# Four shared PSUM banks and other places for attention steps and decoding in a fused attention and Mish-MLP kernel

## The chip, the cores and the metric

The kernel runs on one core of a Trainium2 chip. The metric is the device time of one execution in microseconds (us); each figure for a kernel is the median of several runs. The engines are TensorE (PE, with its weight loads PEld), VectorE (DVE), ScalarE (ACT), GpSimd (POOL) and SyncE (SP), which here only issues DMAs.

## The reference

Four batches of eight heads go through attention with rotary embedding (576 positions, 64 wide). The result, 2304 tokens by 512, goes through two matrix products with h * tanh(softplus(h)), Mish, between them.

```python
q_rot, k_rot = (rotate(q), rotate(k))
scores = scale * np.matmul(q_rot, k_rot.transpose(0, 1, 3, 2))
scores = scores - np.max(scores, axis=-1, keepdims=True)
attn = np.exp(scores)
attn = attn / (np.sum(attn, axis=-1, keepdims=True) + 1e-09)
x = np.matmul(attn, v)            # then (batch, position) x (head, width): 2304 x 512
h = x @ w_in                      # 512 x 2048
sp = np.where(h > 20.0, h, np.log1p(np.exp(np.minimum(h, 20.0))))
return ((h * np.tanh(sp)) @ w_out).astype(np.float32)   # 2048 x 512
```

## The kernel before, in words

Two heads make a pair; there are 16 pairs, four for each batch (pairs 0 to 3 are batch 0). A pair is worked on in five **steps** of 128 queries (the last one has 64 of either head). A step computes scores on PE into tag psc (L494, L488), their maxima on DVE (L502), exp on ACT (L504), and the inverse sums on DVE (L513, L515). For pairs 4 to 15 the weights are split into a high and a low fp16 part (L519 on POOL or L521 on ACT, then L525 on DVE) and transposed by a DMA from SP's queue (L603, L615, L618). For pairs 0 to 3 they stay fp32 and PE transposes them (L537, L550, L554; copies at L544, L545, L558 to L562). The product with V comes for each half of a pair (`av`, L632 to L645; L666, L668 write the fp16 parts of x).

The MLP takes each batch as two **chunks** of 256 and 320 tokens (chunks 0 to 7). A chunk has 16 **units** of 12 matmuls with W_in (`h_unit`, L866) with Mish on ACT (L871), eight splits of the result into fp16 parts (`h_split`, L881 on ACT or L882 on DVE, then L885 on DVE), and 16 **quarter sums** of 12 matmuls with W_out (`p_sub`, L900); four of them fill one output tile (L908).

The weights arrive as 64-bit words and are **decoded** in 32 blocks of 512 columns (`decode`: L762 and L765 or L764, then L768, L771 on DVE, L774, L778), after a scale from the largest exponent has been passed across the partitions by two small matmuls (`max_exponent`, L368, L374). ACT holds either its exp table or its Mish table; each change is an ACT_TABLE_LOAD.

All instructions are recorded first and then put in order by `Plan.order`: a list scheduler that gives each engine its ready instruction of the least priority. The priority is the place in the recorded program, plus shifts (`WSH`, `PSH`), less `ALPHA` times the length of the chain behind it; `DWELL` and `PEN` say how long ACT keeps its table. The recorded program is laid out by tables: `FRONT` attention steps come first, then `SLOTS[c]` names the places in chunk c at which one more step is recorded; `W1L`, `W1S`, `W1D` and `W2L`, `W2D` say at which step the loads, scales and decoding of the quarters of W_in and W_out are recorded, and `PREP`, `PRE0` how long ahead of its first step a pair is loaded.

PSUM has eight banks. Tag psc has two tiles of two banks each. Before, tag ph has two banks (transposes, weight blocks, units of W_in), pp one (sums of W_out, the fifth transposed block, scale exchanges), and po one (products with V). In the last two chunks every second unit and output tile also uses psc and po.

## Time and profile before

| | |
|---|---|
| median of 3 runs | 687.98 us (687.70 to 688.62) |
| the profiled execution's own time | 690.88 us |
| its span, first to last instruction | 688.7 us |
| PE busy | 605.8 us |
| ACT busy | 482.1 us |
| DVE busy | 445.5 us |
| POOL busy | 264.3 us |
| mean granted TensorE clock | 0.958 |

A share of busy time is a mean over stages with different limits, so a table of windows says more than the page's first lines. In it PEclk is the granted TensorE clock as a share of full speed. A wait names the instruction that sat idle and the one that released it. Lines such as L504 are lines of the kernel before.

### The profile page before, as it was taken

The page shows a single profiled execution, that of the slowest core. Times are in us where ns is not written, and L with a number is a line of the kernel's source. Part 1 is how long each engine was busy: PE and PEld are TensorE (multiplying, and loading weights), DVE is VectorE, ACT ScalarE, POOL GpSimd, SP SyncE. Part 2 cuts the span into 40 slices and gives each one's busy share as a digit, 9 for nine tenths or more (in the row PEclk, how much of TensorE's full clock was granted, in tenths as well). Part 3 has the DMA queues.
Part 4 walks back from the last instruction along what each step waited for, and adds up shares of the span by engine and source line. Part 5 has one row for each costly group of instructions (what it writes and reads, how often), then busy time and mean ns, then how long its engine had stood idle before and what let it go on. Part 6 is the DMA issues. An engine that isn't in the chain of part 4 may idle for free.

```text
span 688.7 us, 13057 instructions
## 1 busy us (share of the span) xinstructions
PE 605.8 (88%) x5028; PEld 448.4 (65%) x5028; DVE 445.5 (65%) x984; ACT 482.1 (70%) x864; POOL 264.3 (38%) x247
## 2 busy tenths in 40 slices
PE   1587688768998998968889999998999999999997
PEld 1354355545676676647778777677787767888775
DVE  4899897794887787676757767776767467211110
ACT  3587788764789897647999987779967756442420
POOL 5588734246354537566234546541212001000000
PEclk9868898899999999989999999999999999999999
DMA  9954423242269456896548465755365337100000
GB/s 364 421 188 129 152 68 97 86 147 70 81 142 213 82 119 148 180 202 156 89 88 180 111 121 134 165 88 106 61 122 82 80 62 153 32 2 16 16 11 29
DMA packets 143533, 82.50 MB, mean 120 GB/s; under 512 B 129264, under 2 KB 133488, under 8 KB 141936
## 3 DMA queue, kind: packets, MB, share of 16 engines
q1 hardware_dynamic: 138864, 76.96, 45.5%
q10 hardware_dynamic: 4608, 4.72, 2.0%
q8 instruction: 39, 0.64, 0.4%
q14 instruction: 22, 0.18, 0.1%
HBM read 45.09 MB, written 4.72 MB: 72 GB/s over the span
## 4 chain that ended last, share of the span: by engine, by line
PE 41%; ACT 8%; DMA 7%; DVE 3%; issue 1%; SPq 1%; POOL 1%; ACTq 0%; DVEq 0%; POOLq 0%
PE pp L900 15%; PE ph L866 12%; DMA et<-ew 5%; PE psc L494 4%; PE po L900 3%; PE psc L866 3%; PE po L644 2%; ACT e L504 2%; DMA stg<-in_vflat 1%; ACT L504 1%; ACT L871 1%; DVE ew L525 1%; DVE mx L502 1%; ACT mh L871 1%; PE po L640 1%
## 5 line engine op out<-in xcount | busy, mean ns | idle before, releaser
L866 PE MATMUL ph<-xt,w 128*128 128x256 f16 (+1 forms) x1344 | 180.8, 291 | 13.5 <-ACT mh L871 10.8
L866 PEld LDWEIGHTS <-w 128*128 128x128 f16 x1536 | 149.9, 99 | 59.5 <-issue 18.5
L900 PE MATMUL pp<-g,w 128*128 128x256 f16 (+1 forms) x1344 | 178.0, 287 | 1.9 <-ACT ot L908 1.8
L900 PEld LDWEIGHTS <-w 128*128 128x128 f16 x1536 | 148.0, 98 | 44.9 <-issue 7.9
L504 ACT ACTIVATE e<-psc,mx 128x576 f32<-128x576 f32 x144 | 105.5, 736 | 26.9 <-DVE mx L502 23.6
L502 DVE TENSOR_REDUCE mx<-psc 128x1 f32<-128x576 f32 x144 | 103.7, 750 | 31.3 <-PE psc L494 28.1
L525 DVE SCALAR_TENSOR_TENSOR ew<-e,rs,ew 128x576 f16<-128x576 f32 x108 | 100.3, 945 | 29.2 <-POOL ew L519 20.0
L519 POOL TENSOR_SCALAR ew<-e,rs 128x576 f16<-128x576 f32 x62 | 50.0, 811 | 178.7 <-DVE rs L515 108.4
L494 PE MATMUL psc<-qk 64*128 64x288 f32 (+1 forms) x736 | 90.6, 368 | 27.8 <-ACT qk L420 16.3
L398 POOL TENSOR_TENSOR raw<-raw,cs 128x576 f32<-128x576 f32 x60 | 91.2, 1535 | 58.3 <-DMA raw<-in_qk 55.6
L885 DVE SCALAR_TENSOR_TENSOR g<-mh,cells,g 128x512 f16<-128x512 f32 (+1 forms) x64 | 57.2, 894 | 75.0 <-ACT g L881 74.6
L494 PEld LDWEIGHTS psc<-qk 64*128 64x128 f32 (+1 forms) x736 | 60.2, 199 | 50.7 <-ACT e L504 17.2
L871 ACT ACTIVATE mh<-ph,cells 128x256 f32<-128x256 f32 (+1 forms) x112 | 53.2, 497 | 32.6 <-PE ph L866 31.9
L504 ACT ACT_TABLE_LOAD x43 | 55.2, 1283 | 7.2 <-DVE mx L502 6.5
L871 ACT ACT_TABLE_LOAD x44 | 56.5, 1283 | 1.2 <-ACT ot L908 0.4
L521 ACT ACTIVATE ew<-e,rs 128x576 f16<-128x576 f32 x46 | 35.1, 773 | 31.2 <-DMA et<-ew 22.8
L513 DVE TENSOR_SCALAR sm<-sm 128x1 f32<-128x1 f32 x144 | 21.2, 149 | 42.4 <-ACT e L504 42.0
L778 POOL TENSOR_TENSOR w<-mr,w 128x512 f16<-128x512 f32 x24 | 28.1, 1175 | 48.1 <-ACT w L774 48.0
L402 POOL TENSOR_TENSOR raw<-raw 128x288 f32<-128x288 f32 x48 | 45.2, 958 | 0.1
L645 PE MATMUL po<-et,v 128*64 128x256 f16 (+1 forms) x288 | 42.1, 299 | 0.0
L644 PE MATMUL po<-et,v 128*64 128x256 f16 (+1 forms) x288 | 42.1, 299 | 0.0
L537 PE MATMUL ph<-ident,e 128*128 128x128 f32 (+1 forms) x160 | 25.9, 299 | 15.1 <-ACT e L504 9.0
(113 smaller groups left out, 750.9 us busy)
## 6 DMA issues: line engine op xcount, KB each, us to landing
raw<-in_qk SPq DMA_DIRECT2D x32, 576.0 KB, 4.4
w<-in_w_in SPq DMA_DIRECT2D x4, 1024.0 KB, 12.6
stg<-in_v SPq DMA_DIRECT2D x12, 320.0 KB, 3.4
stg<-in_vflat SPq DMA_DIRECT2D x9, 384.0 KB, 3.4
w<-in_w_out SPq DMA_DIRECT2D x3, 1024.0 KB, 6.3
out_dram<-ot ACTq DMA_DIRECT2D x16, 160.0 KB, 2.1
g<-in_w_in SPq DMA_DIRECT2D x2, 1024.0 KB, 9.3
xt<-in_w_out SPq DMA_DIRECT2D x2, 1024.0 KB, 4.9
```

Of the source, the lines that this page charges most:

```text
L398: e.tensor_tensor(out=t()[:, :, s], in0=t()[:, :, s], in1=cs()[:, :, s], op=ALU.mult)
L402: e.tensor_tensor(out=to, in0=t()[:, 0, s], in1=t()[:, 1, s], op=ALU.add)
L494: nc.tensor.matmul(out, x[own, q], y[own, s], **kw)
L502: op((DVE, dve_ns(S), lambda: nc.vector.tensor_reduce(m(), pt()[:, :, :HS], axis=AX.XY, op=ALU.max, negate=True)), w=[m], r=[pt])
L504: op((ACT, act_ns(S, psum=True, ptr=2), lambda: nc.scalar.activation(e().rearrange("p (c s) -> p c s", c=2), pt()[:, :, :HS], AF.Exp, bias ...
L519: op([(POOL, 1.27 * S, lambda: nc.gpsimd.tensor_scalar(w()[:, c], e(), r()[:, h:h + 1], 1.0, op0=ALU.mult, op1=ALU.mult), 1), (ACT, act_ns ...
L525: op((DVE, dve_ns(S) + 61, lambda: nc.vector.scalar_tensor_tensor(out=w()[:, c], in0=e(), scalar=r()[:, h:h + 1], in1=w()[:, hc], op0=ALU. ...
L644: nc.tensor.matmul(po()[0:64, :n], V()[:, vi, c, 0:64], et[:, c, :], start=False, stop=last)
L866: nc.tensor.matmul(hp(), w1()[:, wi, cc, f:f + 128], x()[:, xi, cc, q0:q0 + n], start=cc == 0 and a == 0, stop=cc == NCC - 1 and a == 2)
L871: op((ACT, act_ns(n, psum=True, ptr=1), lambda j=j, hp=hp: nc.scalar.activation(hn()[:, j, :n], hp(), AF.Mish, scale=uh())), w=[(hn, j)], ...
L885: op((DVE, dve_ns(2 * n) + 61, lambda: nc.vector.scalar_tensor_tensor(out=g()[:, 1, f, :n], in0=hn()[:, :, :n], scalar=f32(gs), in1=g()[:, ...
L900: nc.tensor.matmul(pp()[:, :n], w2e[e]()[:, wi, f], g()[:, gi, f % 8, :n], start=f == 0 and a == 0, stop=f == NF - 1 and a == 2)
```

## The change

The tags ph, pp and po go. Four tiles of one bank each are made once (`bank0` to `bank3`), and `bank()` hands out one of them when the plan issues the first instruction that uses it: the one whose last user ends first by the plan. Units of W_in and weight blocks ask for `bank(1)`: they are issued only while one more bank than they take is free. A new output tile of W_out waits for the one before it (in chunks 6 and 7 for the one before that), as the single bank of pp made it wait. A decoding step is also held until the buffer that it decodes into is free. The tables have new numbers; where the decoding and the steps come to stand follows from them and from the plan.

```diff
-W1L = [1, 2, 3, 4]
-W1S = [2, 3, 4, 5]
-W1D = [3, 4, 6, 7]
+W1L = [2, 0, 1, 4]
+W1S = [2, 3, 6, 7]
+W1D = [5, 3, 7, 7]
-PRE0 = 2
-WSH = 17
-FRONT = 10
+PRE0 = 0
+WSH = 10
+FRONT = 11
-ALPHA = 26
-SLOTS = [[3, 7, 7, 11, 11, 15, 17, 19, 21, 23, 25, 27, 29, 30],
+ALPHA = 36
+SLOTS = [
+    [1, 8, 9, 12, 13, 17, 20, 21, 23, 27, 28, 31],
...
-DWELL = 2000
-PEN = 20
+DWELL = 2251
+PEN = 8
...
+    def pick(self, tag, keep=0):
+        b = Buf(lambda: self.free[tag][b.slot]())
+        b.ring = tag, keep
+        return b
...
         def room(bufs):
+            at = 0.0
+            for tag in {b.ring[0] for b in bufs}:
+                n = sum(b.ring[0] == tag for b in bufs) + max(b.ring[1] for b in bufs)
+                ends = sorted(until(x) for x in held[tag])
+                at = max(at, ends[n - 1])
             return at
...
                     for b in ops[n]["takes"]:
-                        taken[b.ring[0]].append(b)
+                        x = held[b.ring[0]]
+                        b.slot = min(range(len(x)), key=lambda i: until(x[i]))
+                        x[b.slot] = b
...
+    def bank(keep=0):
+        return plan.pick("bank", keep)
...
+    plan.free["bank"] = [Buf(lambda i=i: ps.tile([128, 512], F32, name=f"bank{i}")) for i in range(4)]
...
-            pt = psum((128, 512), "ph", 2)
+            pt = bank()
...
-        po = psum((128, 320), "po")
+        po = bank()
...
-        f, o = psum((128, 512), "ph", 2), row512()
+        f, o = bank(1), row512()
...
-            ph = psum((128, 2, 512), "psc", 2) if wide else psum((128, 512), "ph", 2)
+            ph = psum((128, 2, 512), "psc", 2) if wide else bank(1)
...
         if s == 0:
-            ml["pp"] = psum((128, 320), "po") if c >= 6 and e % 2 else psum((128, 320), "pp")
+            ml["pp"] = bank()
+            sums.append(ml["pp"])
+            ml["pp"].before = sums[-3:-2] if c >= 6 else sums[-2:-1]
```

Three places show how instructions move. The lines of the changed kernel stand 13 lower than those of before from `max_exponent` on (L502 of before is its L515, L768 its L781, L871 its L884), and 15 lower from the sums of `p_sub` on.

**First place: ACT at the start of the program.** The names are qk for the rotated query and key, g and w for the homes of raw weights, ph or bank for PSUM, cells for scales, e for exponentials. Before, and then after:

```order
L994 ACT_TABLE_LOAD
L765 ACTIVATE g_85<-g_85 128x512 x2
L420 ACTIVATE qk<-qk 128x576
L765 ACTIVATE g_87<-g_87 128x512
L504 ACTIVATE e_132,sm<-psc,mx 128x576
L504 ACTIVATE e_136,sm<-psc,mx 128x576
```

```order
L1009 ACT_TABLE_LOAD
L778 ACTIVATE w_69<-w_69 128x512 x2
L775 ACTIVATE bank_76<-w_69,cells 128x512
L775 ACTIVATE bank_77<-w_69,cells 128x512
L433 ACTIVATE qk<-qk 128x576
L787 ACTIVATE w_68<-mr 128x512
L778 ACTIVATE g_94<-g_94 128x512
```

The query's scaling (L420, now L433), which the first scores need, stands behind two weight blocks that are already being decoded with a scale.

**Second place: DVE from the maximum of pair 2's last step on.** The first row is that maximum. The rows go on to the next step's maximum (pair 3, step 2), which comes after 42 rows before and after 16 now. The first twelve of before, and the first twelve after:

```order
L502 TENSOR_REDUCE mx<-psc 128x1
L778 TENSOR_TENSOR w_69<-mr,w_69 128x512
L768 SCALAR_TENSOR_TENSOR ph<-ph,w_69 128x512
L427 SCALAR_TENSOR_TENSOR qk<-raw,qk 128x576
L689 TENSOR_REDUCE cells<-stg 128x1
L885 SCALAR_TENSOR_TENSOR g_1362<-mh,cells,g_1362 128x2x256
L689 TENSOR_REDUCE cells<-stg 128x1
L771 SCALAR_TENSOR_TENSOR mr<-w_69,ph 128x512
L365 TENSOR_REDUCE cells<-cells 128x1
L768 SCALAR_TENSOR_TENSOR ph<-ph,w_69 128x512
L771 SCALAR_TENSOR_TENSOR mr<-w_69,ph 128x512
L721 TENSOR_REDUCE cells<-stg 128x1
```

```order
L515 TENSOR_REDUCE mx<-psc 128x1
L526 TENSOR_SCALAR sm<-sm 128x1
L734 TENSOR_REDUCE cells<-w_69 128x1
L528 RECIPROCAL rs<-sm 128x1
L558 COPY et<-bank_76 128x4x128
L378 TENSOR_REDUCE cells<-cells 128x1
L558 COPY et<-bank_75 128x4x128
L383 TENSOR_REDUCE cells<-bank_76 1x1
L572 COPY et<-bank_77 128x128
L371 TENSOR_SCALAR cells<-cells 1x1
L575 COPY ew<-bank_77 128x128
L371 TENSOR_SCALAR cells<-cells 1x1
```

Decoding (L768, L771, L778) and the MLP's splits (L885) of before stand there no longer; the step's own sums and copies follow at once.

**Third place: ACT in chunk 4.** mh is a unit's Mish, g its split, e an exponential. Before, and then after:

```order
L871 ACTIVATE mh<-ph,cells 128x256 x2
L908 ACTIVATE ot<-pp,cells 128x320
L881 ACTIVATE g_5484<-mh,cells 128x2x256
L504 ACT_TABLE_LOAD
L504 ACTIVATE e_5588,sm<-psc,mx 128x576
L871 ACT_TABLE_LOAD
L871 ACTIVATE mh<-ph,cells 128x256 x2
L504 ACT_TABLE_LOAD
L504 ACTIVATE e_5643,sm<-psc,mx 128x576
L871 ACT_TABLE_LOAD
L871 ACTIVATE mh<-ph,cells 128x256 x2
```

```order
L517 ACT_TABLE_LOAD
L517 ACTIVATE e_5302,sm<-psc,mx 128x576
L517 ACTIVATE e_5331,sm<-psc,mx 128x576
L884 ACT_TABLE_LOAD
L884 ACTIVATE mh<-bank_77,cells 128x256
L884 ACTIVATE mh<-bank_75,cells 128x256
L894 ACTIVATE g_5298<-mh,cells 128x2x256
L884 ACTIVATE mh<-bank_76,cells 128x256
L679 ACTIVATE xt_70<-bank_74 128x320
L894 ACTIVATE g_5298<-mh,cells 128x2x256
L884 ACTIVATE mh<-bank_77,cells 128x256
```

One step's exponentials stand between every two Mish before; now several units follow each other under one table. Over the program ACT has 88 table loads before and 66 now.

## Rows read from the trace of the kernel before

**Rows 1.** The page, part 1: engine, busy us (share of the span), instructions.

```profile
PE 605.8 (88%) x5028; PEld 448.4 (65%) x5028; DVE 445.5 (65%) x984; ACT 482.1 (70%) x864; POOL 264.3 (38%) x247
```

**Rows 2.** Windows: from:to, us, busy of five engines, PEclk, DMA share, GB/s.

```profile
12.50:96.00 83.50, 60.12 (x362) 36.94 (x363) 76.14 (x195) 59.40 (x128) 57.23 (x54) 0.82 0.58 216
96.00:188.00 92.00, 72.70 (x549) 50.39 (x548) 69.51 (x174) 67.23 (x126) 40.39 (x36) 0.93 0.28 92
188.00:303.00 115.00, 105.37 (x896) 75.83 (x895) 86.93 (x191) 92.60 (x168) 63.78 (x55) 0.97 0.69 151
303.00:350.00 47.00, 39.54 (x363) 32.25 (x364) 34.01 (x68) 38.52 (x68) 18.36 (x17) 0.93 0.69 140
350.00:595.00 245.00, 238.01 (x2129) 182.44 (x2129) 162.01 (x337) 191.81 (x326) 78.12 (x76) 1.00 0.53 108
595.00:688.70 93.70, 90.09 (x735) 70.50 (x733) 12.07 (x15) 29.49 (x51) 0.00 (x0) 1.00 0.04 15
```

**Rows 3.** PE's waits, first from 303 to 350, then from 350 to 595 us.

```profile
PE psc L494 <- ACT e L504: 4.4, 3, 2.2
PE ph L866 <- ACT mh L871: 3.4, 4, 1.6
...
PE ph L866 <- ACT mh L871: 4.4, 5, 1.5
```

**Rows 4.** PE's timeline: start, us, engine, line, operation, count [idle before].

```profile
12.52 2.29 PE L494 MATMUL psc<-qk 64*128 64x288 f32 x8 [12.52 <-ACT qk L420]
...
187.94 1.06 PE L494 MATMUL psc<-qk 64*128 64x288 f32 x12
...
303.15 0.40 PE L494 MATMUL psc<-qk 64*128 64x288 f32 x1 [2.25 <-ACT e L504]
...
602.63 2.78 PE L866 MATMUL psc<-xt,w 128*128 128x256 f16 x24
605.26 1.47 PE L866 MATMUL ph<-xt,w 128*128 128x256 f16 x12
```

**Rows 5.** Groups by line: line, engine, operation, shapes, count, busy us, mean ns.

```profile
L768 DVE SCALAR_TENSOR_TENSOR ph<-ph,w 128x512 uint32<-128x512 uint32 x14 | 9.7, 694 | 1.5 <-ACT ph L762 1.5
L771 DVE SCALAR_TENSOR_TENSOR mr<-w,ph 128x512 int32<-128x512 int32 x14 | 9.5, 682 | 0.2
L778 DVE TENSOR_TENSOR w<-mr,w 128x512 f16<-128x512 f32 x8 | 7.1, 883 | 0.9 <-ACT w L774 0.7
L885 DVE SCALAR_TENSOR_TENSOR g<-mh,cells,g 128x512 f16<-128x512 f32 (+1 forms) x64 | 57.2, 894 | 75.0 <-ACT g L881 74.6
L882 DVE TENSOR_SCALAR g<-mh,cells 128x640 f16<-128x640 f32 (+1 forms) x23 | 13.2, 575 | 5.1 <-ACT mh L871 4.0 <-PE pp L900 0.9
L762 ACT ACTIVATE ph<-w,cells 128x512 f32<-128x512 f32 x14 | 9.9, 717 | 0.5 <-DVE et L545 0.3
L871 ACT ACT_TABLE_LOAD x44 | 56.5, 1283 | 1.2 <-ACT ot L908 0.4
L778 POOL TENSOR_TENSOR w<-mr,w 128x512 f16<-128x512 f32 x24 | 28.1, 1175 | 48.1 <-ACT w L774 48.0
```

**Rows 6.** DVE's timeline at two maxima of batch 0.

```profile
137.06 0.75 DVE L502 TENSOR_REDUCE mx<-psc 128x1 f32<-128x576 f32 x1
...
170.78 0.76 DVE L502 TENSOR_REDUCE mx<-psc 128x1 f32<-128x576 f32 x1 [5.57 <-PE psc L494]
```

**Rows 7.** ACT's timeline in chunk 4.

```profile
454.09 1.28 ACT L871 ACT_TABLE_LOAD   x1
455.38 0.84 ACT L871 ACTIVATE mh<-ph,cells 128x256 f32<-128x256 f32 x2
...
456.99 1.28 ACT L504 ACT_TABLE_LOAD   x1
```

**Rows 8.** Windows of line 525 alone: from:to, us, DVE busy (instructions).

```profile
188.00:303.00 115.00, 30.01 (x32) 0.97 0.69 151
350.00:595.00 245.00, 57.94 (x63) 1.00 0.53 108
```

More of the change, by code (lines that the diff above doesn't have):

```diff
@@ L76, in __init__ @@
     def __init__(self):
-        self.ops, self.rings, self.shift, self.free = [], {}, 0, ()
+        self.ops, self.rings, self.shift, self.free = [], {}, 0, {}
     def tile(self, pool, shape, dt, tag, bufs=1):
         ring = self.rings.setdefault(tag, [])
-        free = tag in self.free
-        before = ring[-bufs:][:1] if len(ring) >= bufs and not free else ()
+        before = ring[-bufs:][:1] if len(ring) >= bufs else ()
         ring.append(Buf(lambda: pool.tile(list(shape), dt, name=tag, tag=tag, bufs=bufs), before))
-        if free:
-            ring[-1].ring = tag, bufs
         return ring[-1]
+    def pick(self, tag, keep=0):
+        b = Buf(lambda: self.free[tag][b.slot]())
+        b.ring = tag, keep
+        return b
     def op(self, ways, w=(), r=(), table=None, after=()):
@@ L159, in order, with until @@
         table, since = "exp", 0.0
-        taken, over = {}, {}
+        held, over = {tag: [None] * len(x) for tag, x in self.free.items()}, {}
         def room(bufs):
-            more, at = {}, 0.0
-            for b in bufs:
-                tag, n = b.ring
-                x = taken.setdefault(tag, [])
-                k = len(x) + more.get(tag, 0) - n
-                more[tag] = more.get(tag, 0) + 1
-                if k >= 0:
-                    if not all(done[m] for m in x[k].ops):
-                        return float("inf")
-                    at = max(at, max(over[m] for m in x[k].ops))
-            return at
+            at = 0.0
[3 more added lines that the diff above has]
+                at = max(at, ends[n - 1])
+            return at
+        def until(x):
+            if x is None:
+                return 0.0
+            return max(over[m] for m in x.ops) if all(done[m] for m in x.ops) else float("inf")
         while len(issued) < len(ops):
@@ L312, in attention_mish_mlp @@
     plan = Plan()
-    plan.free = ("ph",)
     op = plan.op
@@ L337, in attention_mish_mlp @@
     xd = [fixed((128, 2, 128), F32R, f"xd{r}") for r in range(2)]
-    for t in (cs, ident, ones, cells, w1, w2, *xt, *xd):
+    plan.free["bank"] = [Buf(lambda i=i: ps.tile([128, 512], F32, name=f"bank{i}")) for i in range(4)]
+    for t in (cs, ident, ones, cells, w1, w2, *xt, *xd, *plan.free["bank"]):
         t()
@@ L360, in ts, with max_exponent @@
         return out
-    def max_exponent(am, cols, lo, hi, bank="po"):
+    def max_exponent(am, cols, lo, hi):
         m = small()
@@ L366, in max_exponent @@
            w=[m], r=[(am, j) for j in range(cols)])
-        pt = psum((128, 320), bank)
+        pt = bank()
         op((PE, 110, lambda: nc.tensor.transpose(pt()[0:1, 0:128], m(), ident())), w=[pt], r=[m, ident])
@@ L372, in max_exponent @@
         e = ts(small((1, 1)), e, lo, hi, ALU.max, ALU.min)
-        pb = psum((128, 320), bank)
+        pb = bank()
         op((PE, 60, lambda: nc.tensor.matmul(pb()[:, 0:1], ones(), e(), start=True, stop=True)), w=[pb], r=[e, ones])
@@ L531, in turned @@
         for h in range(2):
-            pt = psum((128, 512), "ph", 2)
+            pt = bank()
             def fn(h=h, pt=pt):
@@ L545, in turned @@
                 (DVE, dve_ns(4 * n), lambda view=view: nc.vector.tensor_copy(*view()))], w=[(et, (key, h))], r=[pt])
-        pt = psum((128, 320), "pp")
+        pt = bank()
         def both():
@@ L762, in decode @@
         op((ACT, act_ns(512, ptr=1), lambda: nc.scalar.activation(
-            f(), get()[:, :, 1].bitcast(F32), AF.Copy, scale=f32(s)[:, col:col + 1])), w=[f], r=[whole, s], after=[o])
+            f(), get()[:, :, 1].bitcast(F32), AF.Copy, scale=f32(s)[:, col:col + 1])), w=[f], r=[whole, s], after=[o, buf])
         op([(POOL, 1.27 * 512, lambda: nc.gpsimd.tensor_scalar(*bits(), LOW, -0.4999, op0=ALU.mult, op1=ALU.add), 1),
@@ L813, in w2_decode @@
     def w2_decode(q):
-        e = max_exponent(*st["w2", q].amax(), 113.0, 142.0, MEB)
+        e = max_exponent(*st["w2", q].amax(), 113.0, 142.0)
         if q == 0:
@@ L840, in undo_o @@
         sc["uo", b, e] = tiny(u, [a, c], lambda: nc.vector.tensor_scalar(u(), f32(a), c(), None, op0=ALU.mult))
-    ml = {}
+    ml, sums = {}, []
     def h_unit(c, u):
```

27 lines of the change are left out of this document (16 added, 11 removed).

## The prediction

> **What bounds the kernel now.** I read the page's busy shares first, then a table of stages, then who PE waits for, then the places of the steps. PE is busy 605.8 of 688.7 us and ACT 482 [rows 1], so PE is the engine to follow; its shares differ much by stage [rows 2]. I cut the span where PE starts the first scores of pair 4 (187.94, the end of batch 0's attention, the first 12-matmul group) and of pair 8 (303.15, the start of batch 2) [rows 4]. In 12.5 to 188 PE is busy 132.8 of 175.5 us, and in part of it at half clock (mean granted clock 0.82 and 0.93, its levels being 1.2 and 2.4 GHz). DVE is the fullest of the others there, 145.7 of 175.5, ACT has 126.6. In 188 to 303 PE is busy 105.4 of 115, ACT 92.6, DVE 86.9. In 303 to 350 PE has 39.5 of 47 and ACT 38.5. From 350 to 595 PE has 238.0 of 245 at full clock, and after 595 it only lacks the end. So a better order can gain much before 188, some 10 us between 188 and 303, and 14.5 us of idle between 303 and 595; there PE's largest waits are for ACT [rows 3]. PE's own work stays: no matmul is added or taken away.
>
> **The change part by part.**
>
> 1. Edits with one answer. The banks are as many as before (two of tag ph, one pp, one po, now four of one kind), the matmuls the same. A pool cannot hold less than the four fixed places did; what can cost is that each use is bound to a bank when the plan is made, so an instruction can wait for its bank while another lies free. I price this at 0 for the sum: while a weighted sum is open, units had two banks and have two now (one is kept back), and without one they have three. It is in the rivals.
>
> 2. The start. The first load of W_in and its scale chain now go ahead of the first scores on ACT and PE, and the query's load stands behind 2 MB of weights on SP. Before, the first scores start at 12.52, on ACT's L420 [rows 4]. I expect some 5 us later, since L420 now stands behind two L765, two L762 and the wait for the scale. What hides it: DVE and ACT do decoding in the meantime that they otherwise did later, so I cost it at 0; without that cover it is 5.
>
> 3. Batch 0's attention ahead of decoding and MLP units. Ahead of pair 4's first scores there now stand on PE 5 fewer units of W_in and 6 fewer quarter sums of W_out (each 1.31 us: 24 matmuls from 602.63 to 605.26 [rows 4]); on DVE 5 fewer L768 (0.694), 5 L771 (0.682), 6 L778 (0.883), 4 L885 (0.894) and 4 L882 (0.575) [rows 5], which makes 3.5 + 3.4 + 5.3 + 3.6 + 2.3 = 18 us. Some eight array-sized ones more at 0.7 to 0.9 (6 us) go, and three decode steps new on DVE (no such row: bounds 0 and, by L768, 0.7 each) take 2 back: 22. On ACT about 20 fewer, by L762's 0.717 [rows 5] at most 14. The second place in the order listing shows where: between the maxima at 137.06 and at 170.78 DVE had 42 rows and waited 5.57 us for PE [rows 6], and now has 16. If the idle time of the fullest engine stays as it is, pair 4 comes 22 us sooner by DVE, 14 by ACT. I take **-20**, nearer DVE, the fuller one. Bounds: -9 (ACT, with the start's 5 uncovered) and -33 (half of DVE's 22.5 idle us between 96 and 188 going too).
>
> 4. What was left comes between pair 4 and pair 8. PE gets the 11 units (14.4 us) and about 4 us more (an output product of pair 6 and six scale exchanges that now fall here), 18.7 together; ACT gets about 18, since it had 14 less and has 4 more by pair 8 (seven splits are moved onto it from DVE). Its 92.6 of 115 becomes 111 of about 129, DVE's 86.9 about 107, so PE stays the limit. PE's 9.6 idle us of this stage [rows 2] are short waits; with more units to put between scores I let half go. +18.7 - 5 = **+13.7**. Bounds +9 (all idle gone) and +22 (ACT at its present share, worked out under the slower rival).
>
> 5. Table loads. Between pair 8 and the end 22 fewer switches between exp and Mish stand on ACT, at 1.283 us [rows 5]: 28 us less; splits that come over from DVE take some 3 back. Before, in chunk 4 nearly every pair of units is enclosed by two switches: load at 454.09, both Mish at 455.38, load at 456.99 [rows 7]; now up to nine Mish stand in one run (the third place in the order listing). ACT is not the limit over the whole, so this is worth only PE's losses in 303 to 595: idle 7.5 + 7.0, and at most 39.5 x 0.07 = 2.8 by the clock [rows 2]. Of these 4.4 + 3.4 + 4.4 = 12.2 are waits for ACT's exp and Mish [rows 3]. I take **-11**; bounds 0 and -17.3. Next late behind ACT is PE itself.
>
> 6. At the first scores of pair 8 PE has done 2.5 us more than before (two scale exchanges and the output product); so the rest is **-2.5** shorter. The last two chunks keep their order but for one output product.
>
> 7. DVE to GpSimd. Over the program GpSimd gets 6 L778 (1.175 [rows 5]) and about 12 shorter ones, 18 us in all; its share leaves room, 63.8 of 115 us in the fullest late stage. L525 takes 30.01 / 32 = 0.938 us where GpSimd is busy 55% of the time, and 57.94 / 63 = 0.920 where it is 32% [rows 2, 8]. So more GpSimd work costs DVE a few hundredths of a us each, 1 us in all: 0. The Trainium skill, SBUF — State Buffer, "Who interferes with whom", has another rule: a DVE instruction with two SBUF inputs and a GpSimd one that reads SBUF share a port pair, and the second fully blocks. By it the sum would lose up to what GpSimd gets, which is the third rival below; the two rows on L525 bear it out only little.
>
> Sum: -20 + 13.7 - 11 - 2.5 = **-19.8 us**. The profiled span of 688.7 becomes 668.9; the execution itself (690.88, 2.2 us around the span) 671.1. The median of the runs, 687.98, lies 2.9 below that execution, so I predict 687.98 - 19.8 = **668**.
>
> **The rivals.**
>
> - Slower: ACT becomes the limit between pair 4 and pair 8. The start is not covered (step 3 gives -9), then 111 us of ACT work run at the share that the stage has now, 92.6 / 115 = 0.805: 138 us, +22; PE's waits later go only by 3, and -2.5. Together -9 + 22 - 3 - 2.5 = +7.5: 695.5. For: ACT is the fullest engine beside PE there [rows 2], and its waits lie in chains through DVE and PE. Against: between 350 and 595 DVE and ACT keep PE at 238 of 245. It decides from where pair 8's first scores come later than about 308.6 (303.15 + 5.5, which the -3 and -2.5 no longer make up).
> - The same: the work is only moved. Step 3 gives -14, step 4 the whole +18.7, the switches were hidden (-2), -2.5: 688. This is also the case in which the pool does not do what it says, because the bank chosen by the plan is the one that comes free late. For: up to pair 8 the work of PE and ACT is nearly the same in sum. Against: PE's waits for exp and Mish [rows 3] are of the kind that longer runs remove.
> - The shared port: 14 of GpSimd's 18 us fall before pair 8 and hold DVE up on the path: 668 + 14 = 682.
> - Only the late part: steps 3 and 4 cancel, -11 - 2.5: 674.5.
> - More: DVE's saving counts fully, with part of its idle (-27), step 4 at +9, step 5 at -17, -2.5: 687.98 - 37.5 = 650.5. For: the half clock before 188 goes too if PE's gaps there do.
>
> **How the numbers follow.** Forecast 0.47; only the late part 0.17; more 0.14; the port 0.05; the same 0.06; slower 0.11. Within 0.2% (686.6 to 689.4, about what a measurement of this kernel can tell from no change) is the case "the same"; faster are the first four, 0.83. The range leaves out most of the slower case and half of "more": 650 to 690.
>
> **What would show it.** The first scores at about 17 us; pair 4's first scores near 168 and pair 8's near 297; a third fewer decode rows on DVE between pair 2's and pair 3's maxima; about 66 table loads and ACT busy near 457; DVE below 435, GpSimd near 280; PE's idle between pair 8 and the last unit of chunk 5 under 6 us. I am wrong if pair 4 comes after 178 (then DVE was not what held batch 0), if pair 8 comes after 303, if PE's idle after 303 stays at 14 with the table loads gone (then ACT's switches were hidden), or if PE shows new waits of over 10 us in sum for a bank: units, output products or transposes that wait for a reader of the bank they were given.

## The result and the profile after

The changed kernel takes **664.4 us** (median of 4 runs, 662.89 to 668.03) against 688.3 for the kernel before beside it (687.7 to 690.98): ratio 0.965, 95% interval 0.960 to 0.970. That is 3.5% faster; 668 was predicted. The profiled execution took 662.89 us and spans 661.1. The runs' medians and ranges below are of fast executions, which leaves out two slow ones of act_dose_front and one of late_undone.

The page of the changed kernel, part 1 (engine, busy us, share of the span, instructions), answers [rows 1]:

```profile
PE 599.6 (91%) x5028; PEld 445.3 (67%) x5028; DVE 443.1 (67%) x961; ACT 455.6 (69%) x848; POOL 282.5 (43%) x264
```

PE was idle for 688.7 - 605.8 = 82.9 us and now for 661.1 - 599.6 = 61.5, which is 21.4 less; the other 6.2 us are shorter busy time of the same 5028 matmuls. The profiled execution of before is 2.9 us over its kernel's median and this one 1.5 under, so the two differ by 28 us and the medians by 24. To see where, both spans are cut at the same four events: PE's first scores, pair 4's first scores, pair 8's, and the last quarter sum but one of chunk 5 (behind this one three more units of W_in, 36 matmuls, stand now than before). The places, from PE's timeline of the changed kernel (start, us, line, operation), answer [rows 4]:

```profile
17.34 0.85 PE L507 MATMUL psc<-qk 64*128 64x288 f32 x2 [2.27 <-ACT qk L433]
156.80 0.40 PE L507 MATMUL psc<-qk 64*128 64x288 f32 x2
292.26 0.40 PE L507 MATMUL psc<-qk 64*128 64x288 f32 x2
```

The windows between these events (from:to, us, busy of PE, PEld, DVE, ACT, POOL, then PEclk, DMA share, GB/s), first of the kernel before, cut at its own times:

```profile
0.00:12.52 12.52, 0.01 (x1) 0.04 (x1) 4.84 (x6) 3.08 (x4) 6.42 (x10) 1.00 0.86 339
12.52:187.94 175.42, 132.75 (x908) 87.25 (x908) 145.65 (x368) 126.58 (x252) 97.62 (x90) 0.87 0.42 151
187.94:303.15 115.21, 105.43 (x897) 75.89 (x896) 87.08 (x191) 92.81 (x168) 63.78 (x55) 0.97 0.69 152
303.15:589.25 286.10, 271.80 (x2442) 209.83 (x2443) 194.37 (x403) 227.92 (x387) 96.48 (x92) 0.99 0.57 115
589.25:688.70 99.45, 95.84 (x785) 75.35 (x782) 13.58 (x17) 31.75 (x56) 0.00 (x0) 1.00 0.05 15
```

and of the changed kernel:

```profile
0.00:17.34 17.34, 0.95 (x3) 0.58 (x4) 8.52 (x16) 4.67 (x6) 9.05 (x13) 1.00 0.91 366
17.34:156.80 139.46, 112.12 (x759) 71.12 (x760) 124.30 (x301) 108.30 (x226) 90.73 (x87) 0.88 0.45 158
156.80:292.26 135.46, 125.45 (x1072) 91.91 (x1071) 111.47 (x244) 110.82 (x200) 83.48 (x70) 0.97 0.68 157
292.26:557.60 265.34, 261.34 (x2378) 202.79 (x2377) 183.84 (x380) 196.09 (x357) 99.20 (x95) 1.00 0.57 115
557.60:661.10 103.50, 99.77 (x821) 78.87 (x818) 14.98 (x22) 35.68 (x62) 0.00 (x0) 1.00 0.08 22
```

Length less PE's busy time is PE's idle time. It went from 12.5 to 16.4 ahead of the first scores, from 42.7 to 27.3 in the rest of the first stage, from 9.8 to 10.0 between pair 4 and pair 8, from 14.3 to 4.0 after that, and stayed at 3.6 to 3.7 in the last part. So these two executions lose idle time in two places: about 11 us up to pair 4 and about 10 after pair 8.

Only the second place is firm. Each order was profiled once more, the one of before on the shared banks (pool_same_order, median 687.57) and the changed kernel itself (after_again, 666.92). Their windows up to pair 4 and on to pair 8:

```profile
0.00:180.92 180.92, 131.50 (x909) 87.63 (x910) 149.07 (x374) 128.66 (x256) 104.81 (x100) 0.89 0.46 169
180.92:294.68 113.76, 104.88 (x897) 75.85 (x896) 87.33 (x191) 92.90 (x168) 63.65 (x55) 0.97 0.68 152
```

```profile
0.00:156.44 156.44, 112.12 (x764) 71.39 (x764) 133.90 (x316) 113.06 (x233) 99.38 (x99) 0.89 0.50 182
156.44:297.76 141.32, 129.72 (x1072) 94.28 (x1071) 111.30 (x244) 110.77 (x199) 82.84 (x70) 0.94 0.66 150
```

Here PE's idle time up to pair 4 goes from 49.4 to 44.3 us, 5 less and not 11, and pair 8 comes 3 us later (294.68, then 297.76) and not 11 us sooner. After pair 8 the two pairings agree: 385.6 to 368.8 us, and 386.6 to 369.5. So of the 21 to 24 us between the medians 17 come after pair 8, and the 4 to 7 left come before it.

Between the first two stages PE's work only moved. Its groups by line up to pair 4, units of W_in and sums of W_out, before (first two rows) and after:

```profile
L866 PE MATMUL ph<-xt,w 128*128 128x256 f16 x192 | 26.8, 301 | 5.6 <-ACT mh L871 3.0 <-DVE mr L771 2.4 <-DVE et L545 0.2
L900 PE MATMUL pp<-g,w 128*128 128x256 f16 x96 | 11.2, 273 | 0.0
```

```profile
L879 PE MATMUL bank<-xt,w 128*128 128x256 f16 x132 | 15.5, 272 | 1.8 <-DVE ew L575 0.8 <-ACT et L557 0.6 <-DVE et L558 0.3
L915 PE MATMUL bank<-g,w 128*128 128x256 f16 x24 | 2.8, 272 | 0.5 <-ACT mh L884 0.5
```

These groups are 11.3 + 8.4 = 19.7 us shorter in the first stage. They are 132 matmuls fewer, 14.4 us at the 1.31 us for 12 of [rows 4]; the rest is mostly that the matmuls of units took longer before, 301 ns in the mean and now 272. The second stage's busy time rose by 125.45 - 105.43 = 20.0 us.

PE's waits from 292.3 to 557.6 answer [rows 3] (us in total, times, longest):

```profile
PE psc L507 <- ACT e L517: 2.1, 5, 0.8
PE bank L653 <- DMA et<-ew: 1.8, 2, 1.2
PE bank L879 <- ACT mh L884: 0.2, 1, 0.2
```

Units hardly wait for Mish any more (0.2 us). One run of Mish in chunk 4, from ACT's timeline, answers [rows 7]:

```profile
439.30 1.28 ACT L884 ACT_TABLE_LOAD   x1
440.60 0.84 ACT L884 ACTIVATE mh<-bank,cells 128x256 f32<-128x256 f32 x2
441.94 0.47 ACT L884 ACTIVATE mh<-bank,cells 128x256 f32<-128x256 f32 x1
...
449.18 0.48 ACT L884 ACTIVATE mh<-bank,cells 128x256 f32<-128x256 f32 x1 [0.83 <-PE bank L879]
451.00 1.28 ACT L517 ACT_TABLE_LOAD   x1 [0.58 <-DVE mx L515]
```

Nine Mish stand between two loads where there were two.

### The profile page after: what moved, and what is told of

Read it like the earlier page. It is cut to its first block, busy times and chain, and to the rows that moved or that the text cites. A ratio compares the mean times of both kernels' runs of the same rounds, so it can differ in the third digit from the quotient of the medians.

```text
span 661.1 us, 13085 instructions
## 1 busy us (share of the span) xinstructions
PE 599.6 (91%) x5028; PEld 445.3 (67%) x5028; DVE 443.1 (67%) x961; ACT 455.6 (69%) x848; POOL 282.5 (43%) x264
## 5 line engine op out<-in xcount | busy, mean ns | idle before, releaser
L915 PE MATMUL bank<-g,w 128*128 128x256 f16 (+1 forms) x1536 | 201.9, 287 | 2.4 <-DVE g L898 1.2
L915 PEld LDWEIGHTS <-w 128*128 128x128 f16 x1536 | 146.9, 98 | 47.3 <-issue 10.5
L879 PE MATMUL bank<-xt,w 128*128 128x256 f16 (+1 forms) x1344 | 174.4, 286 | 2.5 <-DVE ew L575 0.8
L538 DVE SCALAR_TENSOR_TENSOR ew<-e,rs,ew 128x576 f16<-128x576 f32 x108 | 105.3, 997 | 27.8 <-POOL ew L532 18.2
L517 ACT ACTIVATE e<-psc,mx 128x576 f32<-128x576 f32 x144 | 105.7, 737 | 24.5 <-DVE mx L515 21.4
L532 POOL TENSOR_SCALAR ew<-e,rs 128x576 f16<-128x576 f32 x67 | 54.7, 824 | 157.9 <-DVE rs L528 99.7
L515 DVE TENSOR_REDUCE mx<-psc 128x1 f32<-128x576 f32 x144 | 103.4, 749 | 23.2 <-PE psc L507 19.7
L507 PEld LDWEIGHTS psc<-qk 64*128 64x128 f32 (+1 forms) x736 | 58.0, 189 | 32.3 <-ACT e L517 13.7
L884 ACT ACTIVATE mh<-bank,cells 128x256 f32<-128x256 f32 (+1 forms) x112 | 52.9, 500 | 32.3 <-PE bank L879 31.6
L791 POOL TENSOR_TENSOR w<-mr,w 128x512 f16<-128x512 f32 x30 | 35.9, 1201 | 40.7 <-ACT w L787 32.7
L534 ACT ACTIVATE ew<-e,rs 128x576 f16<-128x576 f32 x41 | 31.3, 774 | 26.6 <-DMA et<-ew 22.0
L894 ACT ACTIVATE g<-mh,cells 128x512 f16<-128x512 f32 (+1 forms) x55 | 42.5, 772 | 4.3 <-PE bank L915 3.3
L923 ACT ACTIVATE ot<-bank,cells 128x256 f32<-128x256 f32 (+1 forms) x32 | 15.9, 496 | 37.1 <-PE bank L915 37.0
L657 PE MATMUL bank<-et,v 128*64 128x256 f16 (+1 forms) x288 | 40.8, 292 | 0.0
## 6 DMA issues: line engine op xcount, KB each, us to landing
g<-in_w_in SPq DMA_DIRECT2D x2, 1024.0 KB, 13.7
```

Source lines behind the costliest of these rows:

```text
L507: nc.tensor.matmul(out, x[own, q], y[own, s], **kw)
L515: op((DVE, dve_ns(S), lambda: nc.vector.tensor_reduce(m(), pt()[:, :, :HS], axis=AX.XY, op=ALU.max, negate=True)), w=[m], r=[pt])
L517: op((ACT, act_ns(S, psum=True, ptr=2), lambda: nc.scalar.activation(e().rearrange("p (c s) -> p c s", c=2), pt()[:, :, :HS], AF.Exp, bias ...
L532: op([(POOL, 1.27 * S, lambda: nc.gpsimd.tensor_scalar(w()[:, c], e(), r()[:, h:h + 1], 1.0, op0=ALU.mult, op1=ALU.mult), 1), (ACT, act_ns ...
L538: op((DVE, dve_ns(S) + 61, lambda: nc.vector.scalar_tensor_tensor(out=w()[:, c], in0=e(), scalar=r()[:, h:h + 1], in1=w()[:, hc], op0=ALU. ...
L879: nc.tensor.matmul(hp(), w1()[:, wi, cc, f:f + 128], x()[:, xi, cc, q0:q0 + n], start=cc == 0 and a == 0, stop=cc == NCC - 1 and a == 2)
```

## Experiments

The runs in one table. PE idle is span less PE's busy time of the profiled execution; "pair 4" and "pair 8" are the starts of their first scores there. "Beside" is the median of the kernel before in the same comparison, all its executions taken.

| run | median us (range) | beside | ratio, 95% | span | PE idle | table loads | pair 4 | pair 8 |
|---|---|---|---|---|---|---|---|---|
| before | 687.98 (687.7-688.62) | | | 688.7 | 82.9 | 88 | 187.94 | 303.15 |
| changed | 664.4 (662.89-668.03) | 688.3 | 0.965 (0.960-0.970) | 661.1 | 61.5 | 66 | 156.80 | 292.26 |
| after_again | 666.92 (665.52-669.03) | 687.99 | 0.968 (0.963-0.972) | 667.3 | 63.6 | 66 | 156.44 | 297.76 |
| pool_same_order | 687.57 (683.47-691.18) | 687.99 | 0.997 (0.994-1.001) | 681.3 | 77.3 | 88 | 180.92 | 294.68 |
| loads_back | 677.99 (676.32-682.4) | 687.99 | 0.986 (0.980-0.991) | 676.6 | 69.9 | 88 | 156.97 | 294.87 |
| late_undone | 683.15 (675.76-684.3) | 687.99 | 0.990 (0.985-0.994) | 682.5 | 75.4 | 106 | 155.17 | 297.60 |
| front_undone | 679.59 (674.61-682.79) | 688.49 | 0.985 (0.979-0.991) | 677.1 | 71.9 | 86 | 142.80 | 296.10 |
| dwell_undone | 682.23 (680.65-683.95) | 689.36 | 0.989 (0.983-0.995) | 679.2 | 73.1 | 92 | 163.69 | 295.75 |
| dve_dose_front | 677.64 (671.92-680.28) | 688.49 | 0.982 (0.976-0.988) | 670.1 | 64.2 | 66 | 162.62 | 301.77 |
| act_dose_front | 683.64 (677.75-687.84) | 688.49 | 0.995 (0.991-0.999) | 676.0 | 66.7 | 66 | 167.28 | 307.65 |
| dve_dose_before | 705.71 (704.75-706.67) | 689.57 | 1.022 (1.017-1.027) | 703.9 | 88.4 | 88 | 205.84 | 318.24 |
| act_dose_before | 705.87 (704.72-709.88) | 689.57 | 1.024 (1.017-1.031) | 702.6 | 87.3 | 88 | 204.06 | 315.68 |
| pool_reads | 672.58 (669.78-673.71) | 688.49 | 0.975 (0.970-0.979) | 670.3 | 64.7 | 66 | 156.89 | 299.36 |
| no_rope_mul | 661.94 (657.27-663.31) | 689.36 | 0.957 (0.950-0.964) | 661.5 | 58.3 | 66 | 156.82 | 293.68 |

How far one profiled execution can be trusted: the changed kernel's two differ by 6.2 us (661.1 and 667.3, granted clock 0.968 and 0.961), 4.1 of it in PE's busy time and 2.1 in its idle time. Between pair 4 and pair 8 after_again takes 5.9 us longer, 4.3 of it in PE's busy time at a granted clock of 0.94 and not 0.97. The kernel before and pool_same_order, whose medians agree, differ by 7 us at pair 4 and 8.5 at pair 8. So differences of places up to pair 8 below some 8 us are not read as effects; the length after pair 8 repeats within 1.1 us.

### The changed kernel again

No edit.

> The changed kernel once more, beside the runs of this call. Expected 662 to 668 us; it is the mark for the kernels that differ from it by one thing.

666.92 us: the gain holds, at 0.968.

### The shared banks alone

The changed code, with the order of every engine written out as it was before; only the bank of each use is chosen anew.

```diff
-        for n, k in self.order():
...
+        for i, (n, e) in enumerate(zip(ORDER[::2], ORDER[1::2])):
...
+                b.slot = min(range(len(x)), key=lambda j: old[j])
```

ORDER is the order of the kernel before, and `old[j]` is the place in it of the last user of bank j.

> The tables and the order of every engine's instructions are those of before; only the banks are the four shared ones, each use taking the bank whose last user stands earliest in that order. By the prediction (the pool alone is worth 0, the places of the work are what counts): 686 to 690 us, ratio to before 0.998 to 1.003. If sharing the banks were itself the gain: below 680.

687.57 against 687.99: no difference (ratio 0.997, interval to 1.001). Four equal banks are worth nothing by themselves that this can tell; what they may do is to allow the other order. The changed order on the old banks was not tried.

### The table loads put back

```diff
+            if (c, u, j) in [(2, 0, 0), (2, 2, 1), ..., (5, 7, 0)]:
+                plan.extra[i] = lambda: nc.scalar.activation(dum[:, 1:2], dum[:, 0:1], AF.Exp)
```

The eleven places lie in chunks 2 to 5, each between two Mish; `plan.extra` is issued right behind the Mish.

> The changed kernel with its order, plus one exp of a single column after 11 of the Mish in chunks 2 to 5 whose next table instruction is another Mish. Each forces two table loads, so ACT again has 88 loads: 22 x 1.283 = 28 us and 11 short instructions more. By step 5 of the prediction (the switches were on PE's path after pair 8, worth 11): pair 8's first scores unmoved and the end 5 to 11 us later, 670 to 676. By the rival (the switches were hidden): within 2 us of the changed kernel, 663 to 667.

Each of the eleven one-element exps brings two loads, 22 in all, and ACT's groups by line show them (count, busy us, mean ns):

```profile
L889 ACT ACT_TABLE_LOAD x44 | 56.5, 1283 | 1.3 <-ACT ot L930 0.4
L522 ACT ACT_TABLE_LOAD x32 | 41.1, 1283 | 5.2 <-DVE mx L520 4.7
L892 ACT ACT_TABLE_LOAD x11 | 14.1, 1283 | 0.2
```

The time is 677.99, which is 11.1 us more than 666.92 beside it, 0.50 us for a load. This is a little over the expected 670 to 676 and far from "hidden". The stage after pair 8 of this run:

```profile
294.87:573.50 278.63, 265.53 (x2377) 204.16 (x2377) 181.22 (x380) 225.27 (x390) 98.64 (x95) 0.99 0.56 109
```

278.63 us instead of 265.34, with 13.1 us of PE idle instead of 4.0, although ACT has 53 us to spare in the stage. The waits of PE's scores and units there for exp and Mish, 2.3 us in the changed kernel, are 9.9 now:

```profile
PE psc L512 <- ACT e L522: 6.2, 8, 2.1
PE bank L884 <- ACT mh L889: 3.7, 4, 1.6
```

From pair 8 to the end this run takes 676.6 - 294.87 = 381.7 us, 12 to 13 more than the changed kernel. The switches were on the path, and 22 of them, put back, cost 11 (by the medians) to 13 of the 17 us that this part had gained.

### The late places as before

```diff
-ALPHA = 36
+ALPHA = 26
...
-DWELL = 2251
-PEN = 8
+DWELL = 2000
+PEN = 20
```

Left out of the cut are the entries of `SLOTS` for chunks 2 to 7, which are as before too.

> The changed kernel with the places of chunks 2 to 7, the weight of the remaining chain and the two table-holding numbers (ALPHA, DWELL, PEN) as before; the front's tables and the banks stay new. ACT has 106 table loads. By the prediction pair 4's first scores stay near 157 to 165 and the part after pair 8 takes 380 us or more, as before (385): 675 to 685. If the late tables give nothing: 662 to 668.

683.15, within the expected range, but not by a clean undoing: the planner answers with 106 loads, 40 more than the changed kernel and 18 more than before. Pair 4 starts at 155.17, so the early numbers bring batch 0's attention forward without the late ones. After pair 8 the run takes 682.5 - 297.60 = 384.9 us, as expected and as before. Between pair 4 and pair 8 PE is idle for 18.8 us, with 27 table loads where the changed kernel has 19:

```profile
155.17:297.60 142.43, 123.64 (x1033) 88.84 (x1033) 112.52 (x252) 120.49 (x204) 85.16 (x72) 0.95 0.71 156
```

### The early places as before

```diff
-W1L = [2, 0, 1, 4]
+W1L = [1, 2, 3, 4]
...
-FRONT = 11
+FRONT = 10
...
```

W1S, W1D, VA, W2L, W2D, PRE0, WSH, AVL, PREP, PSH and the first two entries of `SLOTS` go back to their values of before as well.

> Shared banks and the changed places from chunk 2 on, but the numbers that place decoding, weight blocks and MLP units of chunks 0 and 1 among batch 0's attention as before. Theory one (the front's part of the gain comes from batch 0's attention standing ahead of MLP work, and about half of it is given back up to pair 8): pair 4's first scores at 178-190, pair 8's at 298-306, the time 672-680. Rival (the front gives nothing at the end, all of the gain is in the late part): 662-668. Rival (the two parts only work together): 684 or more.

The time, 679.59, is in the range of theory one, but its mechanism is refuted: pair 4 starts at **142.80**, earlier than in any other run, not at 178 to 190. The late numbers alone (`ALPHA`, `DWELL`, `PEN` hold for the whole program) also bring attention forward. The next stage shows that an early pair 4 is no gain in itself:

```profile
142.80:296.10 153.30, 130.08 (x1059) 94.24 (x1058) 112.53 (x253) 129.18 (x222) 92.94 (x78) 0.92 0.64 154
```

PE is idle for 23.2 us there (10.0 in the changed kernel), with 28 table loads instead of 19 and ACT busy 129.18 of 153.30 us. Pair 8 comes at 296.10. With 86 loads the run has 20 more than the changed kernel, 10 us at the 0.50 of loads_back, by an estimate; the other 2 to 4 us of its loss (by the ratios) stay unexplained.

### Two planner constants as before

```diff
-DWELL = 2251
-PEN = 8
+DWELL = 2000
+PEN = 20
```

> The changed kernel with only the two numbers as before that say how long ScalarE keeps one function table (2000 instead of 2251) and what an operation of the other table must have in due time to break in (20 instead of 8); shared banks and all places of decoding and MLP units as changed. The order then holds 91 table loads in place of 65. Theory one (what a load costs is what the run with 22 loads put back showed, 11 us for 22, thus 0.5 us each, and the places of the units give the rest): 26 loads by 0.5 us are 13 us, the time 677-683. Rival (the gain is in the places alone, loads are hidden): 663-670. Rival (places and table choice pay only together): 686 or more.

92 loads (26 more) and 682.23, 15.3 us over after_again: theory one, at 0.59 us for a load here. From pair 8 to the end, with 20 of the 26, it takes 679.2 - 295.75 = 383.5 us, 14 more than the changed kernel. The planner moved early work too (pair 4 is at 163.69), so the places are not wholly held fixed.

### A dose on VectorE and one on ScalarE, in both orders

Behind the maxima of pairs 0 to 3, 36 reductions into an unused column; behind their exps, 144 small copies:

```diff
+        if front:
+            plan.extra[n] = lambda: nc.vector.tensor_reduce(dum[:, 0:1], cs()[:, 0], axis=AX.X, op=ALU.max)
```
```diff
+        if front:
+            plan.extra[n] = lambda: [nc.scalar.activation(dum[:], cs()[:, 0, 0:32], AF.Copy) for _ in range(4)]
```

> The kernel before, in its own order and banks, with the 36 added reductions on VectorE behind the row maxima of pairs 0 to 3 (0.74 us each, 26.7 us as measured). Theory one (step 3 of the prediction: before, VectorE's row held batch 0): pair 4's first scores move from 181-188 us to 203-215, and the time rises by 15 to 27 us to 703-715. Rival (the chain of maximum, exponent, weights and transposes paces batch 0, and VectorE has idle time beside it, as in the changed kernel, where the same dose moved pair 4 by 6 us): pair 4 at 187-198, the time 690-702.

> The kernel before with four small copies on ScalarE (128 x 32, 0.23 us each as measured) behind each exponent of pairs 0 to 3, 32.8 us. Theory one (VectorE held batch 0, ScalarE had slack): pair 4's first scores move by under 10 us, less than by the dose on VectorE; the time 688-697. Rival (ScalarE paced batch 0): pair 4 moves by 20 us or more, the time 705-720. Rival (a chain through both): by 8 to 15 us, about as in the changed kernel (10.5 us), the time 697-708.

> The changed order with 36 added reductions on VectorE, one behind each row maximum of pairs 0 to 3 (each reads 128 x 576 of the rotary table and writes one unused column; about 0.75 us each by the 128x576 rows, 27 us together). Theory one (step 3 of the prediction: up to pair 4 the kernel waits for VectorE's row): pair 4's first scores move from 156.8 to 177-184 us, and the time rises by 10 to 25 us to 675-690. Rival (VectorE has slack there, what sets pair 4 is ScalarE's exponents or TensorE's own work): pair 4 at no more than 166, the time within 5 us of the changed kernel's, 663-670.

> The changed order with four small copies on ScalarE (128 x 32 each, about 0.16 us) behind each exponent of pairs 0 to 3, 144 in all, about 23 us. Theory one (VectorE's row sets the pace of batch 0, ScalarE has slack): pair 4's first scores move by less than 10 us, to under 167, the time stays at 663-670. Rival (ScalarE's exponents set the pace): pair 4 at 172-182, the time 675-690. Both doses moving pair 4 by more than 15 us would say that the two engines take turns in one chain (maximum, exponent, weights) and neither has slack.

The doses as measured in the kernel before, on DVE and on ACT:

```profile
L510 DVE TENSOR_REDUCE dum<-cs 128x1 f32<-128x576 f32 x36 | 26.7, 741 | 0.0
```

```profile
L513 ACT ACTIVATE dum<-cs 128x32 f32<-128x32 f32 x144 | 32.7, 227 | 3.4
```

In the kernel before, 26.7 us on DVE cost 705.71 - 689.57 = 16.1 us (0.60 for each us), and 32.7 us on ACT cost 16.3 (0.50); pair 4 comes 17.9 and 16.1 us later. Theory one holds for DVE's dose (pair 4 at 205.84, time 705.71), but ACT did not have the slack that it claims: its 16.1 us at pair 4 lie just over the 8 to 15 expected of a chain through both engines and under the 20 of ACT alone. So neither engine held batch 0 alone: a step goes from maximum to exp to weights through both.

In the changed kernel pair 4 moves by only 5.8 us with DVE's dose and by 10.5 with ACT's, in profiled executions that are the fastest of their four and ten. The spans of these two are 2.8 to 9.0 and 8.7 to 14.9 us over those of the changed kernel's two, so within one execution the time rises about as far as pair 4 moves. The medians rise further, by 10.7 and 16.7 over after_again. For DVE's dose neither theory fits: the median rises more than "slack on DVE" allows, and pair 4 moves less than "pace" does. For ACT's dose the time fits "pace", and pair 4 (167.28) lies between the two. I don't take prices from these two runs: a stop of DVE of 7.4 us at 47 us, the subject of the last section, stands in the changed kernel and not in the two dosed ones.

### GpSimd work added and taken away

```diff
+        if h == 0:      # behind the low-part subtraction of the weights
+            plan.extra[n] = lambda: nc.gpsimd.tensor_scalar(cs()[:, 0], cs()[:, 0], 1.0, 1.0, op0=ALU.mult, op1=ALU.mult)
```
```diff
-                e.tensor_tensor(out=t()[:, :, s], in0=t()[:, :, s], in1=cs()[:, :, s], op=ALU.mult)
+                if P < NP:
+                    e.tensor_tensor(out=t()[:, :, s], in0=t()[:, :, s], in1=cs()[:, :, s], op=ALU.mult)
```

The second edit leaves out the product with the rotary table on GpSimd for pairs 4 to 15, so that run computes something else, and only its time is used.

> The changed order with 54 added GpSimd multiplications of a slice of the rotary table by 1.0 (SBUF to SBUF, about 0.8 us each, some 43 us), each behind a low-part subtraction of the weights on VectorE, thus beside VectorE's next work. Theory one (rows of before: a VectorE row that reads SBUF beside GpSimd is 945 to 1000 ns instead of some 900, not stopped): the low-part rows' mean rises by under 60 ns from 997, the time stays at 663-670. Rival (shared port, one engine stops while the other reads): the mean rises by 150 ns or more, VectorE's busy time rises by 15 us or more, the time is 672-690.

> The changed order without the 54 or so multiplications with the rotary table on GpSimd for pairs 4 to 15 (this leaves out that rotary product for these pairs; the additions behind it and all else stay): about 60 us of GpSimd's 282 go. Theory one (GpSimd beside VectorE lengthens VectorE's SBUF rows and costs the kernel about 0.1 us for each us of GpSimd work, as the run with 43 to 54 us added showed 5 to 7 us): the low-part rows' mean falls from 997 to 930-970 ns, the time falls by 3 to 8 us to 657-663. Rival (only the chain behind raw scores counts, and VectorE's longer rows lie beside TensorE's work): the rows shorten, the time stays within 2 us of 664-667.

DVE's low-part rows in the changed kernel, with the added GpSimd work, and with less of it (count, busy us, mean ns, idle before):

```profile
L538 DVE SCALAR_TENSOR_TENSOR ew<-e,rs,ew 128x576 f16<-128x576 f32 x108 | 105.3, 997 | 27.8 <-POOL ew L532 18.2 <-ACT ew L534 9.2
```

```profile
L543 DVE SCALAR_TENSOR_TENSOR ew<-e,rs,ew 128x576 f16<-128x576 f32 x108 | 114.3, 1079 | 32.3 <-POOL ew L537 23.2 <-ACT ew L539 8.8
L547 POOL TENSOR_SCALAR cs<-cs 128x576 f32<-128x576 f32 x60 | 54.2, 904 | 0.7
```

```profile
L539 DVE SCALAR_TENSOR_TENSOR ew<-e,rs,ew 128x576 f16<-128x576 f32 x108 | 98.3, 931 | 24.3 <-POOL ew L533 16.3 <-ACT ew L535 7.7
```

54.2 us of added rows on GpSimd made the mean 82 ns longer, which lies between the two theories (60 and 150), and the time 672.58: by the ratios 0.007 to 0.010 more than the changed kernel's two, 5 to 7 us (the intervals of the ratios overlap in part). About 77 us less (282.5 to 205.9) made the mean 66 ns shorter and the time 661.94, by the ratios 6 to 7.5 us less, by the medians 2.5 to 5; here the intervals overlap too, so the size is open. A us of GpSimd work costs this kernel 0.03 to 0.12 us by these two. Whether through DVE's longer rows or because GpSimd's own later rows are delayed, they don't separate.

## Why the prediction was right, and where it was not

**The sum.** Predicted -19.8 us, measured -23.6 to -23.9 by the medians, and -21.1 in after_again. The terms, by the two profiled executions, with the pairing of pool_same_order and after_again behind the semicolon:

| step | predicted | measured | |
|---|---|---|---|
| 1, the pool | 0 | 0 | pool_same_order |
| 2, the start | first scores 5 later, covered | 17.34 - 12.52 = +4.8 | pair 4 came earlier all the same |
| 3, up to pair 4 | -20 | 156.80 - 187.94 = -31.1; -24.5 | under-sized by 4 to 11 |
| 4, pair 4 to pair 8 | +13.7 | 135.46 - 115.21 = +20.2; +27.6 | under-sized by 7 to 14 |
| 5 and 6, after pair 8 | -13.5 | 368.84 - 385.55 = -16.7; -17.1 | near |
| 7, DVE to GpSimd | 0 | inside the others | missed |

**Steps 3 and 4** have the right sign. Their sum, -6.3 as predicted, is -10.9 in one pairing of traces and +3.1 in the other; the medians less the part after pair 8 leave -4 to -7. So the sum came out near, but the split was wrong: each term was too small, with opposite signs, and that the two errors cancelled is luck. Step 3 was worked out by DVE's lost work, with the idle time of the fullest engine left as it was. DVE's busy time up to pair 4 fell by 17.7 us (150.49 in the trace of before, 4.84 + 145.65, to 132.82), near the 18 to 22 of the prediction; its idle time fell by 13.5 besides (9.3 in the other pairing), where step 3 had left it as it was. On PE the same step reads as 19.7 us less busy time, most of it work that went elsewhere and is no gain, and 5 to 11 us less idle time, which is the gain. The doses on the kernel before show that the premise "DVE holds batch 0" is about half true (0.60 for each us, ACT 0.50). What filled the rest of the idle time isn't settled: the two ways of undoing a part both let the planner change the early order too. In step 4 half of PE's 9.6 idle us was to go; they stayed (9.8 to 10.0, and 8.9 to 11.6 in the other pairing), and PE's busy time rose by 20.0 us (24.8) instead of 18.7. That term is mis-sized by the assumption that more units between scores fill short waits, and in the second pairing by the clock, 0.94 there.

**Step 5** is borne out best: 66 table loads as predicted, ACT busy 455.6 (457 predicted), PE's idle after pair 8 down by 10.2 (11.3 in the other pairing), and loads_back returns 11.1 us for the same 22 loads, in the stage and through the waits that step 5 named. PE's busy time after pair 8 fell by 6.5 us besides (271.80 + 95.84 to 261.34 + 99.77): 2.5 are step 6, and the clock, 0.99 in that stage before and 1.00 now, accounts for up to 3 more. GpSimd's 282.5 and the 4.0 idle us of PE between pair 8 and the last sums of chunk 5 are as foretold (280, under 6).

**Step 7** is the step whose mechanism failed. It read the shared port from means over stages, 0.938 and 0.920 us, as a slight slowing, and priced 1 us. DVE's busy time did not fall to under 435, it is 443.1 for 23 fewer instructions. The low-part rows alone became 5.0 us longer ([rows 8] show parts of the 100.3 that they had in all), and one tiny row of the scale chain takes 7.43 us. The mean hid two kinds of row, untouched and stopped, as the last section shows. So the rival "shared port" had the mechanism; its price of 14 us was too high. By pool_reads and no_rope_mul, 18 us of GpSimd work cost some 0.5 to 2 us, an estimate, so step 7 had about the right price for a wrong reason. What the 7.43 us row costs the kernel was not measured.

**The other rivals.** "Slower" asked for pair 8 after 308.6; it came at 292.26 and 297.76, so it is out. (Its step 4 is 138 - 115 = 23 and not 22, which changes nothing.) But that step 4, ACT's 111 us at the share of before, came near the measured 135.46 and 141.32: ACT was busy for 110.82 of 135.46, 0.82. PE's own work with its old idle time gives about the same length, and the runs don't tell the two apart. "The same" asked for hidden switches; loads_back refutes it. "Only the late part" is not told from the forecast by pair 8, which stood at 303.15 and 294.68 with the old order; against it speaks that the medians moved 4 to 7 us more than the part after pair 8, and that late_undone, whose part after pair 8 is as long as before, still has a ratio of 0.990 (0.985 to 0.994). "More" needed PE's short waits between pair 4 and pair 8 to go, and they stayed. No new wait for a bank appeared: PE's waits for those who read banks into et, mh, ew and mr are 10.7 us in sum over the whole span, in no group over 1.8, where the same kinds made 25.0 before; some of that is data. PE's longest single wait after the first scores, 5.27 us, is that behind the stopped row.

## What to carry to other kernels

When a schedule moves work between stages, price the stage by the bounding engine's idle time: what it takes along as work it has to do elsewhere, and an earlier milestone says nothing by itself (front_undone had pair 4 earliest and was 13 us slower than the changed kernel). A table switch on an engine that has 50 us to spare in a stage can still cost half a microsecond, if the bounding engine's next input stands behind it; put some back to see. And look at the longest single rows beside the means: an average of 997 ns was about 811 for 66 of 108 rows and up to 1967 for the others.
